# Fox attention with a fused MLP: the value product as column tiles side by side, numerators normalised straight out of PSUM

## The chip, the cores and the metric

One core of a Trainium2 chip. The metric is device time of one execution in microseconds (us). The span of a profiled run goes from its first to its last instruction; its clock is the mean share of full speed that TensorE was granted, and 1.0 is full. TensorE is PE, its weight loads PEld, VectorE DVE, ScalarE ACT, GpSimd POOL. All runs compared here are of the fast state, and ratios use those only. A ratio is the mean time of one kernel's fast runs over that of the other's of the same rounds, so it is not quite the ratio of the medians that are quoted.

## The reference, cut to what matters

```python
# q, k, v: (8, 8, 576, 64), f: (8, 8, 576)
scores = np.matmul(q, k.transpose(0, 1, 3, 2)) / np.sqrt(D)
cum = np.cumsum(np.log(np.clip(f, 0.0001, 1.0)), axis=-1)
scores = np.where(causal, -1e9, scores + cum[..., :, None] - cum[..., None, :])
attn = np.exp(scores - scores.max(-1, keepdims=True))
attn = attn / (attn.sum(-1, keepdims=True) + 1e-09)
x = np.matmul(attn, v)            # -> (8 * 576, 512), heads side by side
h = x @ w_in                      # 512 x 2048
out = gelu_tanh(h) @ w_out        # 2048 x 512
```

## The kernel before

Four heads are a *quad*; a quad is scored in a step of four rounds. In round r of a step, PE scores quad i, then makes the value product of one head of the quad before it (j), then a few of the output matmuls of an earlier batch element, which fill PE while ACT and DVE work. With scores held as keys by queries, the decay of the keys is folded into V (`make_vaug`, on POOL), and two extra blocks of 32 columns beside V's 64 make the row sums (denominators) in the same matmul. So a head needs one stationary operand of 128 columns and seven matmuls, 1600 moving columns in all.

```python
    rounds = [
        (0, [(0, 0, 400)]),
        (400, [(0, 400, 176), (3, 384, 192)]),
        (768, [(1, 128, 448)]),
        (1216, [(2, 256, 320), (4, 512, 64)]),
    ]
# ...
    def make_vaug(i):
        va = v_aug[i % 2].rearrange("p t (x y) c -> p (t x) (y c)", y=2)
        va = va.rearrange("p m (e c) -> p m e c", c=64)
        w = wT[:, i, :, :].rearrange("p t (x y) -> p (t x) y", y=2)
        for x in range(2):
            hx = 4 * (i % QPB) + 2 * x
            nc.gpsimd.tensor_mul(
                va[:, x:2 * NT:2, 0:4:3, :], v_nat[(i // QPB) % 2][:, :, hx:hx + 2, :],
                w[:, x:2 * NT:2, :].unsqueeze(3).to_broadcast([128, NT, 2, D]))

        nc.gpsimd.tensor_copy(va[:, :, 1:3, 0:64:32],
                              w.unsqueeze(3).to_broadcast([128, 2 * NT, 2, 2]))
# ...
    def mask(i, r):
        p = pt[i % 2]
        for (t, q0, nq) in rounds[r][1]:
            if q0 == 128 * t:
                o = strip_off[t]
                w = min(128, nq)
                nc.vector.tensor_mul(p[:, :, o:o + w], p[:, :, o:o + w],
                                     utri[:, :, :w].to_broadcast([128, 4, w]))
# ...
    def attn_out(i, h, spare=False):
        if spare:
            po = psS.tile([128, 2, 512], FP32, name="ps_o", tag="s").rearrange("p a n -> p (a n)")
        else:
            po = psO.tile([128, 1024], FP32, name="po", tag="po")
        p, va = pt[i % 2], v_aug[i % 2]

        for t in (0, 1, 3, 2, 4):
            for (a, z, base) in po_parts:
                s = max(a, 128 * t)
                if s >= z:
                    continue
                nc.tensor.matmul(
                    po[:, base + s - a:base + z - a],
                    va[:, t, h, :],
                    p[:, h, strip_off[t] + s - 128 * t:strip_off[t] + z - 128 * t],
                    start=(t == 0), stop=(t == (1 if z == 256 else 4)),
                    skip_group_check=True,
                )
        b, u, x, y = i // QPB, i % QPB, h // 2, h % 2
        if y == 0:
            pair[0] = num_pool.tile([128, S], FP32, name="num", tag="num")
            pair[1] = den_pool.tile([128, S], FP32, name="den", tag="den")
        num, den = pair
        mine, other = slice(64 * y, 64 * y + 64), slice(64 - 64 * y, 128 - 64 * y)
        nc.vector.transpose(out=den[mine, :], in_=po[other, 256:256 + S])
        nc.scalar.copy(num[mine, :], po[mine, 256:256 + S])
        if y == 1:

            rec = den_pool.tile([128, S // 32], FP32, name="rec", tag="rec")
            nc.vector.reciprocal(rec, den[:, 0:S:32])
            rb = den_pool.tile([128, S], FP32, name="rb", tag="rb")
            nc.vector.transpose(out=rb.rearrange("p (c j) -> p c j", j=32),
                                in_=rec.unsqueeze(2).to_broadcast([128, S // 32, 32]))
            nc.gpsimd.tensor_mul(xT[b % 2][:, 2 * u + x, :], num, rb)
# ...
    def step(i, j, fill, per_round, n=None):


        for r in range(4):
            if i is not None:
                score_round(i, r)
                if i == 0 and r == 0:
                    make_w()
            if j is not None:
                attn_out(j, r, spare=(i is None and r % 2 == 1))
            if r == 0:
                if n is not None:
                    cast_k(n)
                    cast_q(n)
                if i == 0:
                    w_in_dmas.append(load_w_in(0))
                if i is not None:
                    make_vaug(i)
            if n is not None:
                if r == 1:
                    transpose_k(n)
                if r == 2:
                    transpose_q(n)
            if i is not None and r > 0:
                mask(i, r - 1)
            pull(fill, per_round)
            if i is not None and r == 3:
                mask(i, 3)
```

The tile `po` has a single buffer (two banks of PSUM). `xT`, the normalised attention output, is the moving operand of the MLP's first matmuls (`ps_h`); the output matmuls are `pso`.

The softmax here doesn't subtract the row's maximum and nothing guards it: scores larger than these inputs give would overflow.

Of the kernel before, what the change touches and what calls it, by code (L numbers as in the profile page):

```python
# [16 lines left out]
def kernel(  # L17
# [10 lines left out]
    nc = tc.nc  # L28
# [33 lines left out]
    ostage_pool = ctx.enter_context(tc.tile_pool(name="ostage", bufs=3))  # L62
    num_pool = ctx.enter_context(tc.tile_pool(name="num", bufs=3))
    den_pool = ctx.enter_context(tc.tile_pool(name="den", bufs=2))
# [18 lines left out]
    kT = many(2, [128, SPAD, 2], BF16, "kT")  # L83
    v_aug = many(2, [128, NT, 4, 128], BF16, "v_aug")
    pt = many(2, [128, 4, PT_COLS], BF16, "pt")
# [6 lines left out]
    before = singles.tile([128, (NT - 1) * BH], FP32, name="before")  # L92
    wT = singles.tile([128, NQ, NT, 4], FP32, name="wT")
    shift = singles.tile([128, 1], FP32, name="shift")

# [61 lines left out]

    def make_vaug(i):
        va = v_aug[i % 2].rearrange("p t (x y) c -> p (t x) (y c)", y=2)
        va = va.rearrange("p m (e c) -> p m e c", c=64)  # L160
        w = wT[:, i, :, :].rearrange("p t (x y) -> p (t x) y", y=2)
        for x in range(2):
            hx = 4 * (i % QPB) + 2 * x
            nc.gpsimd.tensor_mul(
                va[:, x:2 * NT:2, 0:4:3, :], v_nat[(i // QPB) % 2][:, :, hx:hx + 2, :],
                w[:, x:2 * NT:2, :].unsqueeze(3).to_broadcast([128, NT, 2, D]))

        nc.gpsimd.tensor_copy(va[:, :, 1:3, 0:64:32],
                              w.unsqueeze(3).to_broadcast([128, 2 * NT, 2, 2]))

# [29 lines left out]

    pair = [None, None]

    def attn_out(i, h, spare=False):
        if spare:
            po = psS.tile([128, 2, 512], FP32, name="ps_o", tag="s").rearrange("p a n -> p (a n)")
        else:
            po = psO.tile([128, 1024], FP32, name="po", tag="po")
        p, va = pt[i % 2], v_aug[i % 2]

        for t in (0, 1, 3, 2, 4):  # L210
            for (a, z, base) in po_parts:
                s = max(a, 128 * t)
                if s >= z:
                    continue
                nc.tensor.matmul(  # L215
                    po[:, base + s - a:base + z - a],
                    va[:, t, h, :],
                    p[:, h, strip_off[t] + s - 128 * t:strip_off[t] + z - 128 * t],
                    start=(t == 0), stop=(t == (1 if z == 256 else 4)),
                    skip_group_check=True,  # L220
                )
        b, u, x, y = i // QPB, i % QPB, h // 2, h % 2
        if y == 0:
            pair[0] = num_pool.tile([128, S], FP32, name="num", tag="num")
            pair[1] = den_pool.tile([128, S], FP32, name="den", tag="den")
        num, den = pair
        mine, other = slice(64 * y, 64 * y + 64), slice(64 - 64 * y, 128 - 64 * y)
        nc.vector.transpose(out=den[mine, :], in_=po[other, 256:256 + S])  # L228
        nc.scalar.copy(num[mine, :], po[mine, 256:256 + S])  # L229
        if y == 1:  # L230

            rec = den_pool.tile([128, S // 32], FP32, name="rec", tag="rec")
            nc.vector.reciprocal(rec, den[:, 0:S:32])  # L233
            rb = den_pool.tile([128, S], FP32, name="rb", tag="rb")
            nc.vector.transpose(out=rb.rearrange("p (c j) -> p c j", j=32),  # L235
                                in_=rec.unsqueeze(2).to_broadcast([128, S // 32, 32]))
            nc.gpsimd.tensor_mul(xT[b % 2][:, 2 * u + x, :], num, rb)  # L237

# [41 lines left out]
    def setup():  # L280
# [18 lines left out]
        for t_ in v_nat:  # L299
            nc.vector.memset(t_[64:128, NT - 1, :, :], 0.0)  # L300
        nc.vector.memset(v_aug[0], 0.0)
        nc.scalar.activation(f_sb, f_sb, AF.Ln)
# [13 lines left out]
        for t in range(1, NT - 1):  # L316
            nc.vector.tensor_add(before[:, t * BH:(t + 1) * BH],
                                 before[:, (t - 1) * BH:t * BH],
                                 logfT[:, t * BH:(t + 1) * BH])
        nc.vector.memset(v_aug[1], 0.0)  # L320

    def make_w():
# [17 lines left out]

    def step(i, j, fill, per_round, n=None):


        for r in range(4):
            if i is not None:
                score_round(i, r)
                if i == 0 and r == 0:
                    make_w()
            if j is not None:
                attn_out(j, r, spare=(i is None and r % 2 == 1))  # L350
            if r == 0:
                if n is not None:
                    cast_k(n)
                    cast_q(n)
                if i == 0:
                    w_in_dmas.append(load_w_in(0))
                if i is not None:
                    make_vaug(i)
            if n is not None:
                if r == 1:  # L360
                    transpose_k(n)
                if r == 2:
                    transpose_q(n)
            if i is not None and r > 0:
                mask(i, r - 1)
            pull(fill, per_round)
            if i is not None and r == 3:
                mask(i, 3)
# [15 lines left out]
    with tc.manual_schedule():  # L384
        setup()
        step(0, None, none, 0, n=1)
        w_in_dmas.extend(load_w_in(c) for c in range(1, 4))
        qk2 = load_qk(2)
        after(qk2[0], w_in_dmas[2])
        step(1, 0, none, 0)  # L390
        w_out_dmas = [load_w_out(c) for c in range(2)]
        v1 = load_v(1)
        after(v1[0], w_out_dmas[0])
        load_qk(3)
        step(None, 1, none, 0)
        fill = none
        for b in range(B):

            mlp_in(b, (0, 1))
            for x in fill:  # L400
                pass
            if b == 0:
                prepare(2)
                for c in range(2, 4):
                    load_w_out(c)
                load_v(2)
            else:
                prepare(2 * b + 3, 2 * b + 4)
                if b + 2 < B:
                    load_v(b + 2)  # L410
            for ft in range(2, N_FT):
                mlp_in(b, (ft,))
            fill = mlp_out(out_tiles(b))
            if b == 0:
                step(2, None, fill, 7, n=3)
                load_qk(5)
                step(3, 2, fill, 4, n=4)
                load_qk(6)
                step(4, 3, fill, 3)
            elif b + 1 < B:  # L420
                i = 2 * b + 3
                per_round = 7 + 2 * (b % 2)
                pull(fill, 3)
                step(i, i - 1, fill, per_round)
                if i + 1 < NQ:
                    step(i + 1, i, fill, per_round)
                else:
                    step(None, i, fill, 5)
                    pull(fill, 6)
        for x in fill:  # L430
# [31 lines left out]
```

## Time and profile before

| | before |
|---|---|
| time, median (range) | 405.51 us (405.42 to 406.0, 3 runs) |
| span of the profiled run, mean granted PE clock | 404.6 us, 0.952 |
| two batch elements in the steady part (starts of two MLP blocks, 241.18 and 330.00 us) | 88.8 us |
| one head's value product, start to next group's start | 0.70 us |

The page first: busy time and share of the span of each engine, and the two groups of the causal mask (busy us, mean ns of one | idle time before them).

```profile
PE 354.4 (88%) x2825; PEld 209.4 (52%) x2825; DVE 199.2 (49%) x295; ACT 244.2 (60%) x340; POOL 135.0 (33%) x127
...
L198 DVE TENSOR_TENSOR pt_94<-pt_94,utri 128x512 bf16<-128x512 bf16 (+1 forms) x40 | 36.8, 952 | 3.2 <-ACT pt_94 L189 3.2
...
L198 DVE TENSOR_TENSOR pt_95<-pt_95,utri 128x512 bf16<-128x512 bf16 (+1 forms) x40 | 28.8, 746 | 0.0
```

PE is the engine to relieve, either by less array work or by less waiting. Its waits, from the list of waits for PE (who waited for whom: us in total, times, longest):

```profile
PE po L215 <- DVE pt_95 L198: 14.1, 16, 1.1
PE po L215 <- ACT num L229: 5.9, 9, 1.6
...
PE po L215 <- DVE pt_94 L198: 3.7, 4, 1.8
...
PE ps_h L248 <- POOL xT_97 L237: 2.8, 3, 1.5
PE ps_h L248 <- POOL xT_96 L237: 2.5, 5, 1.2
```

The largest is the value product waiting for masks: 14.1 + 3.7 = 17.8 us. The timeline of a step's start in the steady part shows how one comes about (start us, us, engine, line, operation, xcount [idle before <- releaser]):

```profile
311.82 1.43 POOL L237 TENSOR_TENSOR xT_96<-num,rb 128x576 bf16<-128x576 f32 x1 [5.00 <-DVE rb L235]
312.09 0.69 PE L215 MATMUL po<-pt_95,v_aug_93 128*128 128x256 bf16 x5
312.51 2.30 DVE L198 TENSOR_TENSOR pt_95<-pt_95,utri 128x512 bf16<-128x512 bf16 x2
313.21 2.71 POOL L164 TENSOR_TENSOR v_aug_92<-v_nat_87,wT 128x640 bf16<-128x640 f32 x2
313.59 0.30 PE L215 MATMUL po<-pt_95,v_aug_93 128*128 128x320 bf16 x1 [0.81 <-DVE pt_95 L198]
314.86 0.19 PE L215 MATMUL po<-pt_95,v_aug_93 128*128 128x64 bf16 x1 [0.97 <-DVE pt_95 L198]
...
317.36 0.86 PE L215 MATMUL po<-pt_95,v_aug_93 128*128 128x256 bf16 x7
318.06 2.11 PE L266 MATMUL pso<-w_out_sb,gT 128*128 128x512 bf16 x9
```

Two masks take 2.30 us together while POOL multiplies, first xT, then V; a mask with POOL idle takes 0.38 us. The product's last two matmuls, which read the last masked strips, wait 0.81 and 0.97 us. The undisturbed product runs from 317.36 to the next group's start at 318.06: 0.70 us for seven matmuls.

### The profile page before, as it was taken

To read this page: it belongs to the slowest core of one execution; us is meant where nothing else is said; L and a number is where in the kernel's file an instruction comes from. 1 tells how busy PE (TensorE), PEld (TensorE's weight loads), DVE (VectorE), ACT (ScalarE), POOL (GpSimd) and SP (SyncE) were. 2 spreads that over 40 slices of the span, in tenths; PEclk is the share of its full clock that TensorE was granted. 3 is DMA by queue.
4 is the path that set the end of the run, shared out by engine and by line. 5 is a ranking of instruction groups with operands and counts; after the bars stand their busy time and mean duration, and the time that the engine had idled before them with its cause. 6 is when DMAs were issued, how large, how long until landed. Compare 5 with 4: busy or idle time off the path is not lost.

```text
span 404.6 us, 6926 instructions
## 1 busy us (share of the span) xinstructions
PE 354.4 (88%) x2825; PEld 209.4 (52%) x2825; DVE 199.2 (49%) x295; ACT 244.2 (60%) x340; POOL 135.0 (33%) x127
## 2 busy tenths in 40 slices
PE   0546699959899899979999899979999999989996
PEld 0213474425674357535664357535764467546742
DVE  5486613785605772375605682377407660482021
ACT  1735467757577466866577566857676566835600
POOL 2372525551801444051801544143603460121000
PEclk9855799987999999998999999999999999999999
DMA  9998899970493109801592109801640110001012
GB/s 191 173 159 167 149 201 230 230 158 26 113 217 76 53 26 225 153 28 54 127 212 67 52 28 235 142 28 53 170 91 32 50 52 2 28 26 53 0 53 78
DMA packets 86016, 42.55 MB, mean 105 GB/s; under 512 B 40352, under 2 KB 81312, under 8 KB 85984
## 3 DMA queue, kind: packets, MB, share of 16 engines
q1 hardware_dynamic: 79328, 36.73, 41.3%
q0 software_dynamic: 4224, 4.19, 6.7%
q10 hardware_dynamic: 2432, 1.18, 1.4%
q8 instruction: 22, 0.36, 0.4%
q14 instruction: 10, 0.08, 0.1%
HBM read 36.85 MB, written 9.44 MB: 114 GB/s over the span
## 4 chain that ended last, share of the span: by engine, by line
PE 71%; DVE 17%; DMA 4%; POOL 3%; ACT 3%; issue 2%; SPq 0%; POOLq 0%; DVEq 0%; ACTq 0%
PE ps_h L248 29%; PE pso L266 25%; PE po L215 11%; PE ps_s L180 6%; DVE pt_95 L198 5%; DVE den L228 4%; DVE rb L235 3%; DVE pt_94 L198 3%; POOL xT_96 L237 1%; DMA q_nat_81<-in_q_dram 1%; DMA k_nat_82<-in_k_dram 1%; DMA k_nat_83<-in_k_dram 1%; DVE rec L233 1%; POOL xT_97 L237 1%; ACT pt_94 L189 1%
## 5 line engine op out<-in xcount | busy, mean ns | idle before, releaser
L266 PE MATMUL pso<-w_out_sb,gT 128*128 128x512 bf16 x576 | 138.4, 383 | 0.0
L248 PEld LDWEIGHTS <-w_in_sb 128*128 128x128 bf16 x1024 | 100.1, 98 | 35.6 <-issue 7.9
L256 ACT ACTIVATE gT<-ps_h 128x576 bf16<-128x576 f32 x128 | 82.4, 650 | 54.1 <-PE ps_h L248 54.1
L228 DVE STREAM_TRANSPOSE den<-po 64x576 f32<-64x576 f32 x60 | 46.8, 781 | 124.5 <-PE po L215 124.2
L266 PEld LDWEIGHTS <-gT 128*128 128x128 bf16 x576 | 52.4, 98 | 62.5 <-issue 9.5
L248 PE MATMUL ps_h<-xT_96,w_in_sb 128*128 128x288 bf16 x512 | 65.0, 286 | 3.3 <-POOL xT_96 L237 2.5
L248 PE MATMUL ps_h<-xT_97,w_in_sb 128*128 128x288 bf16 x512 | 64.5, 286 | 2.8 <-POOL xT_97 L237 2.8
L229 ACT COPY num<-po 64x576 f32<-64x576 f32 x60 | 37.9, 632 | 42.0 <-DVE den L228 34.6
L189 ACT ACTIVATE pt_94<-ps_s 128x800 bf16<-128x800 f32 (+3 forms) x64 | 50.1, 834 | 20.4 <-PE ps_s L180 20.3
L189 ACT ACTIVATE pt_95<-ps_s 128x800 bf16<-128x800 f32 (+3 forms) x64 | 50.0, 833 | 11.3 <-PE ps_s L180 11.1
L237 POOL TENSOR_TENSOR xT_96<-num,rb 128x576 bf16<-128x576 f32 x16 | 22.8, 1423 | 100.0 <-DVE rb L235 100.0
L237 POOL TENSOR_TENSOR xT_97<-num,rb 128x576 bf16<-128x576 f32 x16 | 22.7, 1421 | 100.0 <-DVE rb L235 100.0
L270 DVE COPY o_st<-pso 128x512 f32<-128x512 f32 x36 | 24.8, 688 | 39.2 <-PE pso L266 38.9
L215 PE MATMUL po<-pt_95,v_aug_93 128*128 128x320 bf16 (+4 forms) x196 | 29.7, 281 | 16.2 <-DVE pt_95 L198 14.1
L215 PE MATMUL po<-pt_94,v_aug_92 128*128 128x320 bf16 (+4 forms) x224 | 30.6, 277 | 9.3 <-ACT num L229 3.9
L198 DVE TENSOR_TENSOR pt_94<-pt_94,utri 128x512 bf16<-128x512 bf16 (+1 forms) x40 | 36.8, 952 | 3.2 <-ACT pt_94 L189 3.2
L215 PEld LDWEIGHTS <-v_aug_93 128*128 128x128 bf16 x224 | 19.8, 104 | 24.5 <-issue 19.2
L215 PEld LDWEIGHTS <-v_aug_92 128*128 128x128 bf16 x224 | 19.2, 102 | 20.3 <-issue 13.8
L198 DVE TENSOR_TENSOR pt_95<-pt_95,utri 128x512 bf16<-128x512 bf16 (+1 forms) x40 | 28.8, 746 | 0.0
L180 PE MATMUL ps_s<-qT_88,kT_90 32*128 32x400 bf16 (+5 forms) x384 | 20.6, 300 | 8.1 <-DVE kT_90 L139 4.5
L235 DVE STREAM_TRANSPOSE rb<-rec 128x576 f32<-128x576 f32 x32 | 24.9, 778 | 2.2
L180 PE MATMUL ps_s<-qT_89,kT_91 32*128 32x400 bf16 (+5 forms) x384 | 20.5, 295 | 1.2 <-DVE qT_89 L139 1.2
(58 smaller groups left out, 187.0 us busy)
## 6 DMA issues: line engine op xcount, KB each, us to landing
out_dram<-o_st SPq DMA_DIRECT2D x36, 256.0 KB, 2.0
k_nat_82<-in_k_dram SPq DMA_DIRECT2D x32, 144.0 KB, 4.8
k_nat_83<-in_k_dram SPq DMA_DIRECT2D x32, 144.0 KB, 3.5
v_nat_87<-in_v_dram SPq DMA_DIRECT2D x16, 256.0 KB, 5.6
q_nat_80<-in_q_dram SPq DMA_DIRECT2D x28, 144.0 KB, 5.2
q_nat_81<-in_q_dram SPq DMA_DIRECT2D x28, 144.0 KB, 4.3
v_nat_86<-in_v_dram SPq DMA_DIRECT2D x12, 256.0 KB, 6.0
w_in_sb<-in_moe_w_in_dram POOLq DMA_DIRECT2D x4, 512.0 KB, 6.4
```

The lines of the kernel that those rows point to most:

```text
L180: nc.tensor.matmul(tiles[h // 2][:, h % 2, c0:c0 + nq], kk[32 * h:32 * h + 32, 128 * t:128 * t + 128, c], qq[32 * h:32 * h + 32, q0:q0 + n ...
L189: nc.scalar.activation(p[:, 2 * g:2 * g + 2, off:off + n], tiles[g][:, :, 0:n], AF.Exp, scale=scale)
L198: nc.vector.tensor_mul(p[:, :, o:o + w], p[:, :, o:o + w], utri[:, :, :w].to_broadcast([128, 4, w]))
L215: nc.tensor.matmul(po[:, base + s - a:base + z - a], va[:, t, h, :], p[:, h, strip_off[t] + s - 128 * t:strip_off[t] + z - 128 * t], start ...
L228: nc.vector.transpose(out=den[mine, :], in_=po[other, 256:256 + S])
L229: nc.scalar.copy(num[mine, :], po[mine, 256:256 + S])
L235: nc.vector.transpose(out=rb.rearrange("p (c j) -> p c j", j=32), in_=rec.unsqueeze(2).to_broadcast([128, S // 32, 32]))
L237: nc.gpsimd.tensor_mul(xT[b % 2][:, 2 * u + x, :], num, rb)
L248: nc.tensor.matmul(ph[:, j, 0:hS], w_in_sb[:, dt, 128 * ft:128 * ft + 128], xT[b % 2][:, dt, hS * j:hS * (j + 1)], start=(dt == 0), stop=( ...
L256: nc.scalar.activation(gT[:, ft, o:o + S].rearrange("p (j n) -> p j n", j=2), ph[:, :, 0:hS], AF.Gelu_apprx_tanh)
L266: nc.tensor.matmul(pso, gT[:, ft, c:c + 128], w_out_sb[:, ft, :], start=(ft == 0), stop=(ft == N_FT - 1))
L270: nc.vector.tensor_copy(st, pso)
```

## The change

The intent is to use the array better. A head's V has 64 columns, so two heads fit side by side as column tiles, each with its own moving operand, and the denominators of four heads fit as four tiles of 32 columns. Three products a quad then replace four. Denominators come first (round 1), their reciprocals are spread over the partitions, and the numerators (rounds 2 and 3) are multiplied on DVE as they leave PSUM; ACT's copy and POOL's multiply go. The loads of w_out and the numbers of fill matmuls per round were rearranged as well. The diff, cut to its core:

```diff
-    def make_vaug(i):
# ... (two multiplies and a copy of 128 x 40 on POOL)
+    def make_vw(i):
+        h0 = 4 * (i % QPB)
+        nc.gpsimd.tensor_mul(
+            vw[i % 2], v_nat[(i // QPB) % 2][:, :, h0:h0 + 4, :],
+            wT[:, i, :, :].unsqueeze(3).to_broadcast([128, NT, 4, D]))
+        nc.gpsimd.tensor_copy(
+            wrep[i % 2], wT[:, i, :, :].unsqueeze(3).to_broadcast([128, NT, 4, 32]))
# ...
-    def attn_out(i, h, spare=False):
# ...
+    def product(i, groups):
+
+        po = psO.tile([128, 1024], FP32, name="po", tag="po")
+        p = pt[i % 2]
         for t in (0, 1, 3, 2, 4):
             for (a, z, base) in po_parts:
                 s = max(a, 128 * t)
                 if s >= z:
                     continue
# ...
+                for (r0, lhsT, h) in groups:
+                    w = lhsT(t)
+                    nc.tensor.matmul(
+                        po[r0:r0 + w.shape[-1], base + s - a:base + z - a], w,
+                        p[:, h, strip_off[t] + s - 128 * t:strip_off[t] + z - 128 * t],
# ...
+    def denominators(i):
+        po = product(i, [(32 * g, lambda t, h=h: wrep[i % 2][:, t, h, :], h)
+                         for g, h in enumerate((0, 2, 1, 3))])
+        den = den_pool.tile([128, S], FP32, name="den", tag="den")
+        nc.vector.transpose(out=den, in_=po)
# ... (two reciprocals, four copies of 32 x 18, two broadcasting transposes into rbs[i, x])
+    def attn_out(i, x):
+        b, u = i // QPB, i % QPB
+        po = product(i, [(64 * y, lambda t, h=2 * x + y: vw[i % 2][:, t, h, :], 2 * x + y)
+                         for y in range(2)])
+        nc.vector.tensor_mul(xT[b % 2][:, 2 * u + x, :], po, rbs.pop((i, x)))
# ... in step():
-            if j is not None:
-                attn_out(j, r, spare=(i is None and r % 2 == 1))
+            if j is not None and r > 0:
+                if r == 1:
+                    denominators(j)
+                else:
+                    attn_out(j, r - 2)
# ...
-            pull(fill, per_round)
+            pull(fill, fills[r])
```

More of the change, by code (lines that the diff above doesn't have):

```diff
@@ L62 @@
     ostage_pool = ctx.enter_context(tc.tile_pool(name="ostage", bufs=3))
-    num_pool = ctx.enter_context(tc.tile_pool(name="num", bufs=3))
     den_pool = ctx.enter_context(tc.tile_pool(name="den", bufs=2))
@@ L83 @@
     kT = many(2, [128, SPAD, 2], BF16, "kT")
-    v_aug = many(2, [128, NT, 4, 128], BF16, "v_aug")
+    vw = many(2, [128, NT, 4, D], BF16, "vw")
     pt = many(2, [128, 4, PT_COLS], BF16, "pt")
@@ L93 @@
     wT = singles.tile([128, NQ, NT, 4], FP32, name="wT")
+    wrep = many(2, [128, NT, 4, 32], BF16, "wrep")
     shift = singles.tile([128, 1], FP32, name="shift")
@@ L156, in transpose_q @@
         transpose_one(q_bf, qT[i % 2])
-    def make_vaug(i):
-        va = v_aug[i % 2].rearrange("p t (x y) c -> p (t x) (y c)", y=2)
-        va = va.rearrange("p m (e c) -> p m e c", c=64)
-        w = wT[:, i, :, :].rearrange("p t (x y) -> p (t x) y", y=2)
-        for x in range(2):
-            hx = 4 * (i % QPB) + 2 * x
-            nc.gpsimd.tensor_mul(
-                va[:, x:2 * NT:2, 0:4:3, :], v_nat[(i // QPB) % 2][:, :, hx:hx + 2, :],
-                w[:, x:2 * NT:2, :].unsqueeze(3).to_broadcast([128, NT, 2, D]))
-        nc.gpsimd.tensor_copy(va[:, :, 1:3, 0:64:32],
-                              w.unsqueeze(3).to_broadcast([128, 2 * NT, 2, 2]))
+    def make_vw(i):
[5 more added lines that the diff above has]
+            wrep[i % 2], wT[:, i, :, :].unsqueeze(3).to_broadcast([128, NT, 4, 32]))
     def score_round(i, r):
@@ L199, in mask @@
                                      utri[:, :, :w].to_broadcast([128, 4, w]))
-    pair = [None, None]
-    def attn_out(i, h, spare=False):
-        if spare:
-            po = psS.tile([128, 2, 512], FP32, name="ps_o", tag="s").rearrange("p a n -> p (a n)")
-        else:
-            po = psO.tile([128, 1024], FP32, name="po", tag="po")
-        p, va = pt[i % 2], v_aug[i % 2]
+    def product(i, groups):
+        po = psO.tile([128, 1024], FP32, name="po", tag="po")
+        p = pt[i % 2]
         for t in (0, 1, 3, 2, 4):
@@ L214, in attn_out @@
                     continue
-                nc.tensor.matmul(
-                    po[:, base + s - a:base + z - a],
-                    va[:, t, h, :],
-                    p[:, h, strip_off[t] + s - 128 * t:strip_off[t] + z - 128 * t],
-                    start=(t == 0), stop=(t == (1 if z == 256 else 4)),
-                    skip_group_check=True,
-                )
-        b, u, x, y = i // QPB, i % QPB, h // 2, h % 2
-        if y == 0:
-            pair[0] = num_pool.tile([128, S], FP32, name="num", tag="num")
-            pair[1] = den_pool.tile([128, S], FP32, name="den", tag="den")
@@ L226, in attn_out @@
-        num, den = pair
-        mine, other = slice(64 * y, 64 * y + 64), slice(64 - 64 * y, 128 - 64 * y)
-        nc.vector.transpose(out=den[mine, :], in_=po[other, 256:256 + S])
-        nc.scalar.copy(num[mine, :], po[mine, 256:256 + S])
-        if y == 1:
-            rec = den_pool.tile([128, S // 32], FP32, name="rec", tag="rec")
-            nc.vector.reciprocal(rec, den[:, 0:S:32])
-            rb = den_pool.tile([128, S], FP32, name="rb", tag="rb")
-            nc.vector.transpose(out=rb.rearrange("p (c j) -> p c j", j=32),
-                                in_=rec.unsqueeze(2).to_broadcast([128, S // 32, 32]))
-            nc.gpsimd.tensor_mul(xT[b % 2][:, 2 * u + x, :], num, rb)
+                for (r0, lhsT, h) in groups:
[3 more added lines that the diff above has]
+                        p[:, h, strip_off[t] + s - 128 * t:strip_off[t] + z - 128 * t],
+                        start=(t == 0), stop=(t == (1 if z == 256 else 4)),
+                        skip_group_check=True,
+                    )
@@ new lines, in product @@
+        return po[:, 256:256 + S]
+    rbs = {}
+    def denominators(i):
[3 more added lines that the diff above has]
+        nc.vector.transpose(out=den, in_=po)
+        rec = [den_pool.tile([128, S // 32], FP32, name=f"rec{x}", tag=f"rec{x}") for x in range(2)]
+        for x in range(2):
+            nc.vector.reciprocal(rec[x], den[:, 0:S:32])
+        for x in range(2):
+            for g in (0, 64):
+                src, dst = g + 32 * x, g + 32 - 32 * x
+                nc.vector.tensor_copy(rec[x][dst:dst + 32, :], rec[x][src:src + 32, :])
+        for x in range(2):
+            rb = den_pool.tile([128, S], FP32, name=f"rb{x}", tag=f"rb{x}")
+            nc.vector.transpose(out=rb.rearrange("p (c j) -> p c j", j=32),
+                                in_=rec[x].unsqueeze(2).to_broadcast([128, S // 32, 32]))
+            rbs[i, x] = rb
@@ L300, in setup @@
             nc.vector.memset(t_[64:128, NT - 1, :, :], 0.0)
-        nc.vector.memset(v_aug[0], 0.0)
         nc.scalar.activation(f_sb, f_sb, AF.Ln)
@@ L319, in setup @@
                                  logfT[:, t * BH:(t + 1) * BH])
-        nc.vector.memset(v_aug[1], 0.0)
     def make_w():
@@ L339, with step @@
     w_in_dmas = []
-    def step(i, j, fill, per_round, n=None):
+    def step(i, j, fill, fills, n=None):
         for r in range(4):
@@ L357, in step @@
                 if i is not None:
-                    make_vaug(i)
+                    make_vw(i)
             if n is not None:
@@ L385 @@
         setup()
-        step(0, None, none, 0, n=1)
+        step(0, None, none, (0, 0, 0, 0), n=1)
         w_in_dmas.extend(load_w_in(c) for c in range(1, 4))
@@ L389 @@
         after(qk2[0], w_in_dmas[2])
-        step(1, 0, none, 0)
-        w_out_dmas = [load_w_out(c) for c in range(2)]
+        step(1, 0, none, (0, 0, 0, 0))
+        w_out_dmas = [load_w_out(c) for c in range(4)]
         v1 = load_v(1)
-        after(v1[0], w_out_dmas[0])
+        after(v1[0], w_out_dmas[1])
         load_qk(3)
-        step(None, 1, none, 0)
+        step(None, 1, none, (0, 0, 0, 0))
         fill = none
@@ L403 @@
                 prepare(2)
-                for c in range(2, 4):
-                    load_w_out(c)
                 load_v(2)
@@ L414 @@
             if b == 0:
-                step(2, None, fill, 7, n=3)
+                step(2, None, fill, (7, 7, 7, 7), n=3)
                 load_qk(5)
-                step(3, 2, fill, 4, n=4)
+                step(3, 2, fill, (7, 3, 3, 3), n=4)
                 load_qk(6)
-                step(4, 3, fill, 3)
+                step(4, 3, fill, (6, 2, 2, 2))
             elif b + 1 < B:
                 i = 2 * b + 3
-                per_round = 7 + 2 * (b % 2)
-                pull(fill, 3)
-                step(i, i - 1, fill, per_round)
+                fills = (11, 8, 8, 9) if b % 2 else (9, 6, 6, 7)
+                pull(fill, 2)
+                step(i, i - 1, fill, fills)
                 if i + 1 < NQ:
-                    step(i + 1, i, fill, per_round)
+                    step(i + 1, i, fill, fills)
                 else:
-                    step(None, i, fill, 5)
-                    pull(fill, 6)
+                    step(None, i, fill, (7, 6, 7, 7))
         for x in fill:
```

## The prediction

> **What bounds it now.** TensorE. In stretches of 45 us from 95 to 365 us PE is busy about 42.6, ACT 30, DVE 23, POOL 16; the chain of waits is 71% PE. The timeline repeats every 88.8 us (two batch elements). In it a head's value product of seven matmuls takes 0.70 us from its start to the next group's, near its streaming time; a score round of 448 columns, two passes, takes 0.50 us, about 0.13 us more than streaming, which I read as the drain between tiling modes. Row tiles do overlap: 16 score matmuls take 0.44 us.
>
> Where PE idles (list of waits): the value product for the causal mask on DVE 14.1 + 3.7 us; for ACT's numerator copy 5.9; the MLP's first matmuls for POOL's xT 5.3. Mask waits come as a pair of 0.8 to 1.1 us at the start of every second step: there a mask takes about 1.15 us, not 0.38, while POOL scales V. The Trainium skill ("SBUF — State Buffer", "Who interferes with whom") says that a VectorE op with two SBUF inputs and a GpSimd op reading SBUF contend; the trace agrees.
>
> **The change.**
> - PE: per quad 4 products of 0.70 us become 3. If column tiles overlap as row tiles do, each is 0.70 to 0.85 us: loads double to 56 a quad, and the Trainium skill ("TensorEngine Tiling (Array Packing)", "Restrictions") says that column tiling disables fast weight load; no trace here shows the cost yet. Estimate: 2.8 us falls to about 2.3. But product and output matmuls no longer share a mode: three more drains of 0.13 us a quad. Net 2 to 4 us in all.
> - The product moves from rounds 0-3 to 1-3, when the last step's masks are done even behind POOL's scaling: most of the 18 us of mask waits, and the half-clock windows after some, go. The largest gain: 10 to 15 us.
> - ACT loses 64 copies of 0.63 us (off the path, but psO comes free sooner: about 5 us). POOL loses 32 products of 1.42 us. DVE: 64 transposes of 0.78 become 16; 32 multiplies out of PSUM of about 0.75 (estimate from the 0.69 us copy of 512 columns) and 64 small copies come: about even.
> - The chain behind a quad's last product shrinks from transpose, reciprocal, transpose, POOL multiply (3.3 us) to one DVE multiply: about 5 us, mostly of xT waits and start-up before 50 us.
> - New: single-buffered psO waits for the DVE multiply, which stands behind about 3.3 us of reciprocal work: up to 0.4 us a quad, about 3 us.
>
> Sum: 3 + 13 + 5 + 5 + 3 (batch 0, last step) - 3 = about 26 us.
>
> **Prediction: 379 us**, 366 to 394 eight times in ten. Faster by over 2%: 0.88; within 2%: 0.05; slower: 0.07.
>
> **What will show it.** A product of 0.7 to 0.85 us in the timeline; two batch elements in 82 to 84 us; waits for masks below 4 us; ACT busy near 205, POOL near 95, DVE near 195 us; xT waits about nil; a new wait of the product for DVE's multiply, below 7 us.
>
> **What would make it wrong.** Column tiles that don't overlap, or weight loads that can't be hidden: a denominator product of 1.5 to 2.8 us and 20 to 60 us lost. Mask waits that only move to round 1. A DVE backlog that delays psO at every quad.

## The result, and the profile after

The change took the time from 405.75 us (405.42 to 406.55, 4 runs) to **381.54 us** (380.64 to 383.2, 4 runs): ratio 0.9405, 95% interval 0.937 to 0.9441. The profiled run spans 378.9 us at a mean clock of 0.98. Two batch elements now take 83.0 us (MLP blocks at 138.99 and 221.98 us).

The page after, the lines that answer to those of before, and one of the output matmuls:

```profile
PE 339.7 (90%) x3235; PEld 203.7 (54%) x3273; DVE 181.6 (48%) x341; ACT 205.9 (54%) x276; POOL 93.2 (25%) x79
...
L271 PE MATMUL pso<-w_out_sb,gT 128*128 128x512 bf16 x538 | 129.2, 381 | 5.1 <-issue 4.6
...
L193 DVE TENSOR_TENSOR pt_92<-pt_92,utri 128x512 bf16<-128x512 bf16 (+1 forms) x40 | 30.9, 798 | 0.0
L193 DVE TENSOR_TENSOR pt_91<-pt_91,utri 128x512 bf16<-128x512 bf16 (+1 forms) x40 | 27.3, 718 | 4.6 <-ACT pt_91 L184 4.6
```

A caution on reading: 576 output matmuls run, the trace has 538, while their 576 weight loads are all there. PE has 38 matmuls fewer than loads. The "issue" time of 4.6 us is where a missing record sat, not idle PE. The list of waits for PE:

```profile
PE po L208 <- DVE xT_94 L242: 4.8, 6, 1.6
PE pso L271 <- issue: 4.6, 28, 0.3
...
PE po L208 <- DVE xT_93 L242: 4.4, 3, 1.8
PE po L208 <- DVE pt_91 L193: 3.6, 3, 2.3
...
PE po L208 <- DVE den L223: 0.9, 1, 0.9
```

Waits for masks fell from 17.8 to 3.6 us, those for ACT's copy and for POOL's xT are gone, and a new one has come: 4.8 + 4.4 + 0.9 = 10.1 us in which the product waits until DVE has emptied `po`. The same kind of stretch as before, a step's start:

```profile
287.45 2.33 POOL L160 TENSOR_TENSOR vw_89<-v_nat_84,wT 128x1280 bf16<-128x1280 f32 x1 [18.36 <-PE po L208]
288.08 1.98 DVE L193 TENSOR_TENSOR pt_92<-pt_92,utri 128x512 bf16<-128x512 bf16 x1
...
290.59 1.56 DVE L193 TENSOR_TENSOR pt_92<-pt_92,utri 128x512 bf16<-128x512 bf16 x2
...
292.73 0.87 PE L208 MATMUL po<-pt_92,wrep_103 128*32 128x256 bf16 x28
...
293.76 1.67 PE L271 MATMUL pso<-w_out_sb,gT 128*128 128x512 bf16 x7 [0.16 <-issue]
...
295.65 0.78 DVE L234 STREAM_TRANSPOSE rb_3889<-rec_3881 128x576 f32<-128x576 f32 x1
295.87 0.88 PE L208 MATMUL po<-pt_92,vw_90 128*64 128x256 bf16 x14
296.36 0.74 DVE L234 STREAM_TRANSPOSE rb_3891<-rec_3882 128x576 f32<-128x576 f32 x1
296.67 1.47 PE L271 MATMUL pso<-w_out_sb,gT 128*128 128x512 bf16 x6
297.01 0.38 DVE L193 TENSOR_TENSOR pt_91<-pt_91,utri 128x512 bf16<-128x512 bf16 x1
297.32 0.75 DVE L242 TENSOR_TENSOR xT_93<-po,rb_3889 128x576 bf16<-128x576 f32 x1
```

The masks are as slow as ever (1.98 us for one, 1.56 us for two, beside POOL), but they end at 292.15 us and the product that reads them starts at 292.73 us, so nobody waits. A product of two 64-column tiles takes 295.87 to 296.67, 0.80 us. The one of four 32-column tiles seems to take 1.03 us to 293.76, but eight output matmuls were issued there and seven are recorded; their pitch is 0.215 us, so the first began at about 293.54 and the product took 0.81 us. The last lines show the new wait in the making: the first numerators stand in `po` from about 296.8 us (an estimate: DVE began to read the denominators 0.93 us after their product's start), but their multiply starts at 297.32, behind two transposes, of which it needs one, and a mask.

Where the 25.7 us of span between the two profiled runs went:

| term | before, us | after, us | change |
|---|---|---|---|
| product waits for masks | 17.8 | 3.6 | -14.2 |
| product waits for ACT's copy out of `po` | 5.9 | 0 | -5.9 |
| product waits for DVE to empty `po` | 0 | 10.1 | +10.1 |
| MLP waits for POOL's xT | 5.3 | 0 | -5.3 |
| product waits for POOL's V (once, at the start) | 1.7 | 0 | -1.7 |
| array time of the products, 16 quads: 4 x 0.70, then 3 x 0.81 (an estimate, all at the full clock) | 44.8 | 38.9 | -5.9 |
| sum | | | -22.9 |

The remaining 2.8 us are not attributed. The mean clock does not explain them: a repeat of the kernel after had 0.959 in place of 0.98, and its span was 378.8 us; two runs of the kernel before with 0.996 span 404.2 and 403.6 us, against 404.6 at 0.952. The rearranged loads of w_out and the other numbers of fill matmuls were not tested by themselves.

### The profile page after: what moved, and what is told of

The parts are those of the page before. It is cut to its first block, busy times and chain, and to the rows that moved or that the text cites. A ratio compares the mean times of both kernels' runs of the same rounds, so it can differ in the third digit from the quotient of the medians.

```text
span 378.9 us, 7775 instructions
## 1 busy us (share of the span) xinstructions
PE 339.7 (90%) x3235; PEld 203.7 (54%) x3273; DVE 181.6 (48%) x341; ACT 205.9 (54%) x276; POOL 93.2 (25%) x79
## 4 chain that ended last, share of the span: by engine, by line
PE 75%; DVE 12%; issue 5%; DMA 4%; ACT 3%; SPq 0%; POOL 0%; ACTq 0%; POOLq 0%
PE ps_h L253 34%; PE pso L271 27%; PE po L208 9%; PE ps_s L175 5%; DVE pt_91 L193 2%; DMA v_nat_83<-in_v_dram 1%; DVE den L223 1%; DMA k_nat_80<-in_k_dram 1%; DVE xT_94 L242 1%; DVE pt_92 L193 1%; ACT pt_92 L184 1%; DMA k_nat_79<-in_k_dram 1%; DVE o_st L275 1%; ACT L184 1%; DVE xT_93 L242 1%
## 5 line engine op out<-in xcount | busy, mean ns | idle before, releaser
L271 PE MATMUL pso<-w_out_sb,gT 128*128 128x512 bf16 x538 | 129.2, 381 | 5.1 <-issue 4.6
L271 PEld LDWEIGHTS <-gT 128*128 128x128 bf16 x576 | 51.6, 98 | 63.8 <-issue 8.4
L223 DVE STREAM_TRANSPOSE den<-po 128x576 f32<-128x576 f32 x16 | 12.5, 783 | 93.8 <-PE po L208 93.5
L193 DVE TENSOR_TENSOR pt_92<-pt_92,utri 128x512 bf16<-128x512 bf16 (+1 forms) x40 | 30.9, 798 | 0.0
L193 DVE TENSOR_TENSOR pt_91<-pt_91,utri 128x512 bf16<-128x512 bf16 (+1 forms) x40 | 27.3, 718 | 4.6 <-ACT pt_91 L184 4.6
L147 POOL CAST k_bf<-k_nat_79 128x1152 bf16<-128x1152 f32 x8 | 9.2, 1148 | 80.5 <-DVE kT_88 L139 60.3
L175 PE MATMUL ps_s<-qT_85,kT_87 32*128 32x400 bf16 (+5 forms) x384 | 21.3, 299 | 7.6 <-DVE kT_87 L139 4.6
L175 PE MATMUL ps_s<-qT_86,kT_88 32*128 32x400 bf16 (+5 forms) x384 | 22.5, 294 | 2.7 <-DVE qT_86 L139 1.2
L160 POOL TENSOR_TENSOR vw_89<-v_nat_84,wT 128x1280 bf16<-128x1280 f32 x4 | 9.3, 2331 | 55.1 <-PE po L208 36.7
L175 PEld LDWEIGHTS <-kT_87 32*128 32x128 bf16 x384 | 8.1, 96 | 24.1 <-issue 17.7
L160 POOL TENSOR_TENSOR vw_89<-v_nat_83,wT 128x1280 bf16<-128x1280 f32 x4 | 9.3, 2335 | 45.2 <-PE po L208 36.1
L208 PE MATMUL po<-pt_91,vw_89 128*64 128x320 bf16 (+4 forms) x224 | 15.2, 278 | 5.1 <-DVE xT_94 L242 3.2
L208 PE MATMUL po<-pt_92,vw_90 128*64 128x320 bf16 (+4 forms) x224 | 15.3, 280 | 4.2 <-DVE xT_93 L242 1.8
L175 PEld LDWEIGHTS <-kT_88 32*128 32x128 bf16 x384 | 8.4, 95 | 19.4 <-issue 17.3
L208 PEld LDWEIGHTS <-vw_89 128*64 128x64 bf16 x224 | 11.5, 115 | 9.3 <-issue 8.4
```

The costliest lines, as they stand in the source:

```text
L147: nc.gpsimd.tensor_copy(k_bf, k_nat[i % 2])
L160: nc.gpsimd.tensor_mul(vw[i % 2], v_nat[(i // QPB) % 2][:, :, h0:h0 + 4, :], wT[:, i, :, :].unsqueeze(3).to_broadcast([128, NT, 4, D]))
L175: nc.tensor.matmul(tiles[h // 2][:, h % 2, c0:c0 + nq], kk[32 * h:32 * h + 32, 128 * t:128 * t + 128, c], qq[32 * h:32 * h + 32, q0:q0 + n ...
L193: nc.vector.tensor_mul(p[:, :, o:o + w], p[:, :, o:o + w], utri[:, :, :w].to_broadcast([128, 4, w]))
L208: nc.tensor.matmul(po[r0:r0 + w.shape[-1], base + s - a:base + z - a], w, p[:, h, strip_off[t] + s - 128 * t:strip_off[t] + z - 128 * t], ...
L223: nc.vector.transpose(out=den, in_=po)
```

## Experiments

The theory (A): most of the gain is idle time of PE that was removed, above all the mask waits, because the product now comes a round later; the array itself gained little, as three products with mode switches cost nearly what four without did. The rival (B): the gain is array time, as the change intended. A second question came with the result: is it good to normalise straight out of PSUM, when `po` then waits for DVE?

Medians below are of different chips and rounds; ratios are each to the kernel before in the same rounds.

| run | median, us | ratio to before (95%) |
|---|---|---|
| before, output matmuls first | 412.12 | 1.0165 (1.0134 to 1.0195) |
| before, V scaled in round 2 | 394.56 | 0.972 (0.9699 to 0.9741) |
| after, one tile at a time | 402.73 | 0.9923 (0.9904 to 0.9943) |
| after, product split by fill | 393.5 | 0.969 (0.9674 to 0.9707) |
| after, again | 380.58 | 0.9374 (0.9349 to 0.9398) |
| after, ACT copy and POOL multiply | 375.5 | 0.9245 (0.9219 to 0.927) |
| after, second pair's reciprocals later | 374.69 | 0.9229 (0.9207 to 0.9252) |
| the last, and V scaled after the masks | 373.36 | 0.9194 (0.9168 to 0.9221) |
| after, denominators in round 0 | 389.31 | 0.9556 (0.953 to 0.9581) |
| after, ACT copy, POOL multiply, V scaled after the masks | **371.44** | 0.9118 (0.9094 to 0.9142) |

All ten gave right results.

### Idle time removed without touching the array

Two edits of the kernel *before*. The first puts the output matmuls ahead of the product in a round:

```diff
+            k = (per_round + 1) // 2 if r == 3 else per_round
+            if j is not None and i is not None:
+                pull(fill, k)
             if j is not None:
                 attn_out(j, r, spare=(i is None and r % 2 == 1))
# ...
-            pull(fill, per_round)
+            pull(fill, per_round - k if j is not None and i is not None else per_round)
```

> The kernel before, full-width products kept; in rounds 0 to 2 the output matmuls of a round go ahead of the value product, in round 3 half of them. Theory A (most of the gain was idle PE time, above all waits for the masks): a product then starts 1.5 to 1.9 us later in its round, so the product's waits for masks fall from 17.8 us to below 10 and the time falls by 6 to 10 us, to about 396 to 400, though nothing on the array has changed; the xT waits may rise by 3 to 6 us. Rival B (the gain was array time saved by column tiles): no change, within 1 us of before.

Measured: 412.12 us, 1.65% slower. Waits for masks fell only to 13.8 us and waits for xT rose to 10.8. The idea was wrong: POOL's work hangs on the last product. In this run's steady part POOL's xT multiply, which normalises that product (225.32 us), and the scaling of V right behind it (226.72 us) run beside three masks that take 3.20 us. Put the products later, and POOL's work and the slow masks move later with them. The last product also stands nearer to the MLP that needs it. The run says nothing for or against rival B; it shows that "later" alone buys nothing. Why the time rose by 6 us, when PE's waits for other engines rose by 4.0 us in sum, is open.

The second leaves the order on PE alone and issues POOL's scaling in round 2 of the step, behind xT multiplies that hold it there:

```diff
-                if i is not None:
+                if i == 0:
                     make_vaug(i)
+            if r == 2 and i is not None and i > 0:
+                make_vaug(i)
```

> The kernel before, but POOL's scaling of V for quads 1 and up is issued in round 2 of a step and no longer in round 0. Theory A, with the two engines contending: the masks at a step's start are then held up by POOL's xT multiply only, waits for masks fall from 17.8 us to about 8 to 12, time 398 to 402. Rival B: no change. If a mask still takes 1.1 us at a step's start with POOL idle, the contention is not the cause.

Measured: 394.56 us, 2.8% faster. The list of waits for PE:

```profile
PE po L215 <- DVE pt L198: 8.4, 10, 1.1
```

At a step's start only the xT multiply now runs beside the two masks, and they take 1.23 us in place of 2.30:

```profile
213.73 1.43 POOL L237 TENSOR_TENSOR xT<-num,rb 128x576 bf16<-128x576 f32 x1 [1.88 <-DVE rb L235]
214.41 1.23 DVE L198 TENSOR_TENSOR pt<-pt,utri 128x512 bf16<-128x512 bf16 x2
```

Moving one POOL call gave about 11.4 us (0.028 x 406.18), 47% of what the whole change gave (1 - 0.9405 = 0.0595, 24.1 us), with every matmul as it was. That is against rival B as the main cause. The slow mask moved with POOL: one in round 2, beside the scaling, now takes 1.26 us (at 223.05 us). The gain was larger than expected (398 to 402), and the fall in mask waits (9.4 us) does not cover all of it.

### Side by side or one after another

The kernel *after*, with the loop over tiles outside the loop over key blocks:

```diff
-        for t in (0, 1, 3, 2, 4):
-            for (a, z, base) in po_parts:
-                s = max(a, 128 * t)
-                if s >= z:
-                    continue
-                for (r0, lhsT, h) in groups:
+        for (r0, lhsT, h) in groups:
+            for t in (0, 1, 3, 2, 4):
+                for (a, z, base) in po_parts:
+                    s = max(a, 128 * t)
+                    if s >= z:
+                        continue
                     w = lhsT(t)
```

> The kernel after, same matmuls and same column tiles, but all seven of one tile before the next tile's. If column tiles overlap only when neighbours in the queue sit in different tiles, a denominator product takes about 4 x 0.67 + 0.13 = 2.8 us in place of 0.81 to its successor's start and a numerator product 1.5: 3.4 us a quad more, 16 quads: about +50 us, 425 to 435 (less 5 to 10 that hides in waits). If the array had run them one after another all along, no change.

Measured: 402.73 us, about 21 us over the kernel after, not 50. Its timeline (the first output matmul after the product of 28 is again missing):

```profile
207.75 1.81 PE L208 MATMUL po<-pt,wrep 128*32 128x256 bf16 x28
209.72 1.67 PE L271 MATMUL pso<-w_out_sb,gT 128*128 128x512 bf16 x7 [0.16 <-issue]
...
211.83 1.20 PE L208 MATMUL po<-pt,vw 128*64 128x256 bf16 x14
212.96 1.90 PE L271 MATMUL pso<-w_out_sb,gT 128*128 128x512 bf16 x8
```

The four tiles took 1.75 us (to 209.72 less one pitch of 0.215) and the two 1.13 us, against 0.81. So overlap is worth what it promises, but the expected sum of the tiles' times, 2.8 us, was wrong. The start times in the trace say why. (The trace does not name the tile of a matmul; it is read here from the column counts and the order of issue in the kernel.) Each tile's matmuls have 256, 320, 128, 320, 192, 320 and 64 columns, in this order; the starts of the 28 matmuls begin so (ns after the first, columns):

```
0 256 | 120 320 | 255 128 | 311 320 | 317 256 | 437 320 | 447 192 | 530 320 | 573 128 | 629 320 | 635 256
```

At 317 ns the second tile's first matmul (256) starts, 6 ns after the first tile's fourth, and the first tile's fifth (192) starts only at 447. PE runs ahead into another tile past matmuls that wait for their own. So tiles overlap at their seams even in the wrong order, by about 0.36 us at a seam: (2.68 + 0.14 - 1.75) / 3, with 2.68 us four times the streaming time of 1600 columns at 0.42 ns (320 columns took 0.134 us).

### What a mode switch costs

The kernel *after*, with half of a round's output matmuls in the middle of the product, none added:

```diff
         for t in (0, 1, 3, 2, 4):
+            if t == 3 and mid is not None:
+                pull(*mid)             # mid = (fill, fills[r] // 2)
# ...
-            pull(fill, fills[r])
+            pull(fill, fills[r] - k)   # k = fills[r] // 2 where a product ran
```

> The kernel after, but half of a round's output matmuls go into the middle of the value product, none added: two more mode switches per product, 42 products have such matmuls. If a switch costs about 0.12 us as the gap over streaming says: +9 to +12 us, 390 to 394. If switches are free and the gaps are pipeline latency that hides: within 2 us of the kernel after. The waits for psO may fall a little, as the product ends later.

Measured: 393.5 us; by ratios 0.969 - 0.9405 = 0.0285 of 406 us, 11.6 us more than after. One product of it in the timeline:

```profile
205.15 0.63 PE L210 MATMUL po<-pt,vw 128*64 128x256 bf16 x8
205.71 1.04 PE L273 MATMUL pso<-w_out_sb,gT 128*128 128x512 bf16 x4
206.68 0.44 PE L210 MATMUL po<-pt,vw 128*64 128x192 bf16 x6
207.05 1.04 PE L273 MATMUL pso<-w_out_sb,gT 128*128 128x512 bf16 x4
```

The first half, 1024 columns in each tile or 0.43 us of streaming, takes 0.56 us to the next start; four output matmuls, 0.86 us by their pitch, take 0.97 us. So a switch costs 0.13 us out of column tiles and 0.11 us into them. Two more for each of 42 products are 10.1 us (an estimate from these two). The 11.6 us measured are not switches alone: the product's waits for DVE to empty `po` rose too, from 10.1 to 14.2 us, probably because a product then has less fill behind it. Without these 4.1 us, 7.5 us are left. So a switch is not free, but the total fixes its mean cost over 84 switches only to 0.09 to 0.14 us. This is what the design pays at each product: 0.67 us of streaming became 0.81.

### Denominators back in round 0

The kernel *after*, with the empty round moved from 0 to 1 (and the fill of the two exchanged):

```diff
-            if j is not None and r > 0:
-                if r == 1:
+            if j is not None and r != (1 if i is not None else 0):
+                if r == (0 if i is not None else 1):
                     denominators(j)
```

> The kernel after, but the denominators go into round 0 of a step and round 1 has none (the numbers of output matmuls of the two rounds change places). Theory A: a product right after the step's start meets masks that POOL's scaling still holds up: waits for masks 3.6 us in the kernel after become 10 to 18 us, time 388 to 394. If the move off round 0 was not what removed them: within 2 us of the kernel after. The reciprocal work then has a round to itself before the first multiply, so the 9.2 us of waits for DVE's multiply fall by up to 6 and could hide part of the loss.

Measured: 389.31 us, ratio 0.9556 against 0.9374 of the kernel after. Waits for masks are back at 13.2 us, in 18 waits. That line, and a step's start:

```profile
PE po L208 <- DVE pt L193: 13.2, 18, 2.3
...
209.66 2.33 POOL L160 TENSOR_TENSOR vw<-v_nat,wT 128x1280 bf16<-128x1280 f32 x1 [18.36 <-PE po L208]
210.29 1.98 DVE L193 TENSOR_TENSOR pt<-pt,utri 128x512 bf16<-128x512 bf16 x1
...
212.80 1.56 DVE L193 TENSOR_TENSOR pt<-pt,utri 128x512 bf16<-128x512 bf16 x2
213.26 0.32 PE L208 MATMUL po<-pt,wrep 128*32 128x320 bf16 x4 [0.47 <-DVE pt L193]
...
214.41 0.21 PE L208 MATMUL po<-pt,wrep 128*32 128x64 bf16 x4 [0.83 <-DVE pt L193]
```

Same POOL multiply, same slow masks (1.98 and 1.56 us) as in the kernel after; now the product is there before they end. This is the test of the largest term of the prediction, and theory A holds: the empty round after POOL's trigger is what removed the mask waits. Waits for DVE's multiply fell too (9.2 to 3.0 us), as expected, and hid part of the loss; one wait of 1.7 us for POOL's `wrep` at the start is new. The first failed edit and this one differ in the point that matters: what seems to count is the time between the product that releases V's buffer and the next product that reads the masks.

### Straight out of PSUM, or through a copy

The anchor for what follows is the kernel after in the same rounds:

> The kernel after, unchanged, as the anchor of this chip: ratio to before 0.937 to 0.944, about 381.5 us.

Measured: 380.58 us, ratio 0.9374. Next, the old way of normalising in the new kernel, so that ACT empties `po`:

```diff
-        nc.vector.tensor_mul(xT[b % 2][:, 2 * u + x, :], po, rbs.pop((i, x)))
+        num = num_pool.tile([128, S], FP32, name="num", tag="num")
+        nc.scalar.copy(num, po)
+        nc.gpsimd.tensor_mul(xT[b % 2][:, 2 * u + x, :], num, rbs.pop((i, x)))
```

> The kernel after, but the numerators are copied out of PSUM by ACT and multiplied on POOL as before; column tiles and rounds stay. If normalising straight out of PSUM is worth much: the xT waits of the MLP come back (about 5 us), POOL's multiplies run against the masks again, 385 to 390. If its gain is paid back in full by psO waiting for DVE's multiply (9.2 us of waits in the kernel after, which fall to about 4 here): within 2 us of the kernel after. I expect 383 to 387.

Measured: 375.5 us, 5 us *faster* than the kernel after. My expectation had the sign wrong. The product's waits for `po` fall from 10.1 us to 2.9 (2.0 for ACT, 0.9 for DVE), and waits of the MLP for POOL's xT come to 0.8 us only, not 5. A likely reason, not tested by itself, is that the reciprocals are ready by then: ACT's copy and POOL's multiply (0.65 + 1.41 us) follow the last product, in place of a chain of 3.3 us. Waits for masks rose to 5.6 us. ACT and POOL had the room: 223.3 and 136.9 us busy. This part of the change, in the order in which it was issued, cost time.

Third, DVE keeps the multiply, but the second pair's reciprocal, copies and transpose come behind the first pair's multiply:

```diff
-        for x in range(2):
-            nc.vector.reciprocal(rec[x], den[:, 0:S:32])
# ... (copies and transposes of both pairs)
+        broadcast(i, 0)      # reciprocal, copies and transpose of the first pair
# ... in attn_out:
         nc.vector.tensor_mul(xT[b % 2][:, 2 * u + x, :], po, rbs.pop((i, x)))
+        if x == 0:
+            broadcast(i, 1)
```

> The kernel after, but reciprocal, copies and broadcast transpose of the second pair of heads are issued on DVE behind the first pair's multiply. If psO waits because the multiply stands behind 3.3 us of reciprocal work: the product's waits for xT on DVE fall from 9.2 us to 3 to 5, time 2 to 5 us less than after (376 to 379). If DVE is full as such and order does not matter: same within 1 us.

Measured: 374.69 us, 5.9 us less than the kernel after. Waits for DVE's multiply fell from 9.2 to 2.3 us while DVE's busy time stayed (182.7 against 180.8 us):

```profile
PE po L208 <- DVE xT L246: 2.3, 4, 0.8
```

So it was the order on DVE, not its load. Normalising out of PSUM is as good as the copy (the intervals of the two ratios overlap), once the multiply is not behind work that it doesn't need.

### The last mask waits

Both of these add one dependency: POOL's scaling for quad i waits for the last mask of quad i - 1.

```diff
+        scaled = nc.gpsimd.tensor_mul(vw[i % 2], ...)
+        if i - 1 in masked:
+            after(scaled, masked[i - 1])     # masked[i]: the last mask of quad i
```

> As e6_second_later, and POOL's scaling of V for a quad also waits for the last mask of the quad before. In the steady part mask waits are nil already, so only start-up and batch 0 can gain: mask waits 3.6 us to below 1, masks at 0.38 to 0.5 us in place of 0.8, time 2 to 4 us below e6_second_later: 373 to 376. If the slow masks at start-up have another cause (DMA), no change.

Measured: 373.36 us, within the range, but only 1.3 us below the run before it: the intervals of the two ratios overlap. Waits for masks are gone from the list, and waits for DVE's multiply rose from 2.3 to 7.6 us. This is the plainest evidence that POOL's scaling makes masks slow: in the run before, 25 of the 80 masks took over 0.6 us and all together 57.3 us; here it is 6, and 34.0 us. Its timeline near the start:

```profile
25.90 2.36 POOL L160 TENSOR_TENSOR vw<-v_nat,wT 128x1280 bf16<-128x1280 f32 x1
...
26.50 2.46 DVE L240 COPY rec<-rec 32x18 f32<-32x18 f32 x2
```

POOL's multiply now runs against two copies of 32 x 18, which take 2.46 us in place of 0.35, and the multiply that frees `po` is behind them. At start-up the collision was not removed, it met another victim. So the last version puts the dependency on the one with ACT's copy, where `po` doesn't hang on DVE:

> As e5_copy_then_pool (ACT empties PSUM, POOL multiplies), and POOL's scaling of V waits for the last mask of the quad before. e5 has 5.6 us of waits for masks left, nearly all before 83 us; with them gone and psO never behind DVE's multiply: waits for masks below 1 us, 370 to 373 us. If the wait just turns into another (the small copies held up by POOL, as in e8): no better than e8, 373 to 375.

Measured: **371.44 us**, ratio 0.9118 to before; against the kernel after, by the two ratios, 0.9118 / 0.9374 = 0.973. This beats both kernels. Its waits for PE:

```profile
PE po L213 <- DVE pt L198: 3.6, 2, 2.3
...
PE ps_h L260 <- POOL xT L249: 0.9, 1, 0.9
PE po L213 <- ACT num L248: 0.7, 1, 0.7
```

The time is as expected, the mask waits are not (below 1 us expected): 3.6 us remain in two waits at the start.

## Why the prediction was right, point by point

- **The time**: 379 predicted, 381.54 measured, range 366 to 394. A sum of terms of about 26 us met 24.1. That it came so close is luck: by the table, the product's wait for DVE was 7.1 us larger than charged, and the array (2.9 us), the masks (1.2), ACT's copy (0.9) and xT (0.3) gave more than credited; the 3 us for start-up and batch 0 can't be checked.
- **Mask waits, 13 us** ("The largest gain"): right. 14.2 us fell away, and putting the denominators back in round 0 brought 13.2 us of waits and about 7 us of time back (0.0182 of 407). That POOL makes the masks slow is shown by the late scaling in the kernel before and by the scaling after the masks.
- **Array time, 3 us**: the mechanism was right, the size too small: 5.9 us by the trace. A product takes 0.81 us, inside the stated 0.70 to 0.85. But that figure contains the switch, and the sum charged "three more drains of 0.13 us a quad" on top. With 4 x 0.70 - 3 x 0.81 = 0.37 us a quad no drain is left to subtract.
- **psO's wait for DVE, 3 us, "below 7 us"**: the mis-sized term on the other side. It was 10.1 us. The cause was named rightly ("stands behind about 3.3 us of reciprocal work") and shown by the order experiment. The size, 0.4 us a quad, fits the steady rounds with much fill. But 8.1 of the 10.1 us fell before 100 us, into start-up and batch 0, where a round has two or three output matmuls or none.
- **ACT's copy 5 us and xT 5 us**: 5.9 and 5.3 us. That both waits vanish was right, but the cause given was in the main wrong. The prediction credited the copies that go ("psO comes free sooner") and the chain that shrinks "to one DVE multiply". With ACT's copy and POOL's multiply put back, those waits come to 2.0 and 0.8 us only, and the run is 5 us faster. The rest must come from what that run keeps: 32 copies in place of 64, and reciprocals that are done in round 1. Which of these did it was not tested.
- **Startup and batch 0, 3 us**: not to be told apart from the other terms in the trace.
- **"the half-clock windows after some, go"**: they went, but their worth is not shown. The trace before has half clock for 6.8 us from 88.9 us and for 3.4 us from 181.1 us, both after waits for masks. After start-up (from 50 us) the profile after has 3.4 us of it, from 80.4 us, and its repeat none until the last instructions; the two have the same span (378.9 and 378.8 us).
- **Busy times**: ACT 205.9 (205 predicted), POOL 93.2 (95), DVE 181.6 (195). DVE fell by 17.6 us, not by 4. What goes and what comes was "about even", as I had said (transposes of the denominators from 49.9 to 12.5 us, against 24.0 of multiplies and 11.4 of copies). But the masks took 7.4 us less (65.6 to 58.2 us in their groups), two clears of V's operand (2.3 us) went, and the reciprocals and the transposes that spread them took 4.2 us less, in part because they now overlap; 1.7 us are left over.
- **The fears**: column tiles do overlap, and the loads are hidden: four tiles with 28 loads and two tiles with 14 take the same 0.8 us.

## What to carry to other kernels

Before crediting a change of array layout with a gain, list the waits that its reordering removes, and try to remove them in the old layout; here one moved POOL call gave nearly half of the gain. When an operation is slow only beside another engine, find what triggers that engine: here the collision moved with its trigger, and taking it off the masks put it, at start-up, on the small copies. An operation that frees a single PSUM buffer must not queue behind work that it doesn't need; move that work behind it, or let an engine with room empty the buffer.

## What the Trainium skill lacked or had wrong

- "TensorE: Matmul & The Clock Gate", "The mechanism", says that matmuls are "strict FIFO, no reordering" in start and end. With the matmuls of one column tile issued before those of the next, the next tile's first matmul started 6 ns after the fourth of the tile before, whose fifth started 130 ns later; four tiles took 1.75 us, not 2.68.
- "TensorEngine Tiling (Array Packing)", "Key Properties", says that changing the tiling mode drains TensorE and gives no figure. The runs show 0.13 us out of column tiles into the full array and 0.11 us back; the run with 84 more switches took 11.6 us longer, 4.1 us of it longer waits for DVE.
- The same page, "Restrictions", says that column tiling disables fast weight load, and gives no cost there. Here a load of 128 x 64 took 0.115 us and one of 128 x 32 0.10 us, against 0.098 us for 128 x 128 in the full array, all hidden behind matmuls. "TensorE: Matmul & The Clock Gate", "LDWEIGHTS (loading the stationary operand)", gives columns / 1.2 ns. For 64 columns that is 53 ns (worked out from the page), less than half of what the records show; for 128 it is 107 ns, near the 98 recorded.
- "SBUF — State Buffer", "Who interferes with whom": the trace agrees that a VectorE op with two SBUF inputs contends with a GpSimd op, and that a copy from SBUF to SBUF can. Durations for these are not there: beside POOL's scaling a mask of 0.38 us took 1.98 us in the steady part and 3.08 us once at start-up, and two copies of 32 x 18 took 2.46 us in place of 0.35.
- No page that I read warns that a missing matmul record looks like 0.16 us of "issue" idle before its successor; 38 of 3273 were missing in the profile after, and the count against the weight loads shows it.
